# Routing steps of the attention stage at one per place instead of two, and the first expert's lower weight quarters all on GpSimd

## The chip, the cores and the metric

One Trainium2 chip, one of its cores. The metric is the device time of one execution in microseconds (us), lower is better. An execution's own time is a little longer than the span of its instructions, since something lies around them.

## What is computed

A linear attention with a per-channel decay (4 batches, 8 heads, 768 positions, 48 channels) whose result, read as 3072 rows of 384 values, goes through two layers of eight experts; each row takes the one expert with the largest logit.

```
for t in range(S):
    state = alpha[:, :, t, :, None] * state + np.einsum('bhd,bhe->bhde', k[:, :, t], v[:, :, t])
    y[:, :, t] = np.einsum('bhd,bhde->bhe', q[:, :, t], state)
...
h = np.maximum(xc[mask] @ w1[e], 0.0)
y[mask] = gate_w[mask, None] * (h @ w2[e])
```

The first layer skips rows whose score `x @ w_skip` is not positive and adds its result to the row; the second takes every row.

## The kernel before, in words

The attention is cut into NB = 24 chunks of 128 positions (6 per batch). The outer loop runs over g = 0 to 23, and an iteration g holds, in program order, work of several chunks:

- `emit_a(g + 1)`: 16 score matmuls of the next chunk into two PSUM banks (`ap`, L575), the causal mask for one bank by VectorE (L583) and for the other by ScalarE and GpSimd (L580, L581), then four transposes of the keys (`kp`, L590), which are left out where g + 1 is the last chunk of a batch.
- `prep(g + 3)`: two scans by VectorE over the decays with a reciprocal between them (L555, L557, L559), then two products by GpSimd (L563, L564).
- `emit_r(g - 1)`: eight matmuls (`rp`, L658) that give the rows and the logits of the chunk before; ScalarE copies the rows out and VectorE adds up the logits (`lg`, L661).
- `emit_y(g)`: the outputs (`yp`), from the masked scores (L612, L613) and from the carried state (L621, L622; left out where g is the first chunk of a batch), and the new state (`sp`, L617, L618, then `sa` by VectorE, L633, and four small copies by ScalarE, L636; left out where g is the last chunk of a batch).

The banks `ap` (two), `rp`, `sp` and `yp` come in turn out of one ring of four PSUM banks (tag "B"). An allocation takes the bank used four allocations earlier, so the second `ap` bank of an iteration is the `rp` bank of the iteration before, and is free once VectorE has made `lg`.

Engines take their instructions in program order. What TensorE runs is written out by hand in that order.

Rows are routed in groups of 6, 6, 6, 3 and 3 chunks (GROUPS). `route(i)` starts once the last chunk of its group has been through `emit_r`, that is in iterations 6, 12, 18, 21 and 23. It is a generator of small steps (softmax, choice of expert, rank within the expert, list of indices), nearly all VectorE instructions of 0.15 to 1 us, and it starts a second generator, `row_ends`, for counts, gates and a DMA of the row ends on SP's queue. `rt(n)` runs n steps, taken in turn from the active generators; `release()` lets a step go on that was left at a `yield 1` (the matmuls of rank, L322 to L325, and of the indices, L386). Calls of `rt` stand between the instructions of the attention: one in `emit_a` behind the mask, three in `prep`, three in `emit_r`, two in `emit_y`, and RT[g] at the end of the iteration (1 up to iteration 15). Two steps are heavy: `mv` (L374) and `hot` (L381), the latter followed by the index matmuls.

`finish` would run what is left of group i - 2 when group i starts.

From iteration 6, every second iteration ends with `background()`, one quarter of a split of the first expert's weights: ScalarE writes the f16 upper part (L205), then VectorE or GpSimd the bf16 lower part (`split_w`, L210). ON_POOL says which quarters GpSimd makes; for expert 0 these are quarters 0 and 2 of each of the two weights, so iterations 6, 10, 14 and 18 put one on GpSimd and 8, 12, 16 and 20 one on VectorE.

Behind the attention come the experts of the first layer and of the second, in which the weights of later experts are loaded into two raw buffers and split while TensorE works on the one before.

Of the kernel before, what the change touches and what calls it, by code (L numbers as in the profile page):

```python
# [47 lines left out]
SPLIT = 3  # L48
NWARM = 13

RT = [1, 1, 1, 1, 1, 1, 1, 1, 1, 1, 1, 1, 1, 1, 1, 1, 0, 2, 0, 2, 10, 10, 7, 14]

TURNS2 = ((0, 3), (1, 1), (1, 5), (2, 1))
REL3 = (2, 1, 3, 3, 3, 3, 3, 1, 1)
# [18 lines left out]
SPLITS2 = (((2, 0), (2, 2), (2, 4), (2, 6)), ((0, 3), (0, 6), (1, 3), (1, 6)))  # L73
TURNS = (((2, 1), (2, 3), (2, 5)), ((0, 1), (1, 1), (2, 1), (2, 4)))

ON_POOL = [(0, 2)] + [(1, 2, 3)] * 8 + [()] * 7

CST = {}
CW = 0
# [31 lines left out]
def body(tc, qka, vN, rw, wg2, wg17, w1a, w2a, w1b, w2b, cst, zr, out):  # L111
# [3 lines left out]
    with ctx:  # L115
# [21 lines left out]
        with ExitStack() as fctx, tc.manual_schedule():  # L137
# [8 lines left out]
            def bank(tag, name, *shape, parts=128):  # L146

                pool, bufs = phase.get(tag, (ps, 1))
                t = pool.tile([128, 512], F32, tag=tag, name=name, bufs=bufs)
                v = t[0:parts, 0:int(np.prod(shape))]  # L150
                if len(shape) == 2:
                    v = v.rearrange("p (a b) -> p a b", a=shape[0])
                elif len(shape) == 3:
                    v = v.rearrange("p (a b c) -> p a b c", a=shape[0], b=shape[1])
                return v
# [43 lines left out]
            def split_w(x, m, s):  # L199
# [5 lines left out]
                A.activation(out=hi[:, sl], in_=r[:, sl], func=AF.Copy)  # L205
                eng = P if s in ON_POOL[x] else V
                if x and s and eng is P and s - 1 not in ON_POOL[x]:

# [22 lines left out]
            def step(r):  # L231
                tok = next(r[0], None)
                if tok is None:
                    active.remove(r)
                else:
                    r[1] = turn[0] + (tok == 3) * LAG if tok in (1, 3) else None
                return tok != 2

            def rt(n=1):
                for _ in range(n):  # L240
                    for r in list(active):
                        if r[1] is None:
                            active.remove(r)
                            active.append(r)
                            if step(r):
                                break

            def release(w=1):
                turn[0] += 1
                for r in list(active):  # L250
                    if r[1] is not None and r[1] < turn[0] - w:
                        step(r)

            def start(gen):
                r = [gen, None]
                active.append(r)
                return r
# [292 lines left out]
            def prep(g, parts):  # L550

                a = at[g]
                pf = wk.tile([GP, AW], F32, tag="pp", name="pp", bufs=4)
                pp = pt[g] = pf.rearrange("p (a c) -> p a c", a=NP)
                V.tensor_tensor_scan(pf, a, bz, initial=0.0, op0=ALU.mult, op1=ALU.add)  # L555
                rt()
                V.reciprocal(bz.rearrange("p (a c) -> p a c", a=NP)[:, :, C + 1:], pp[:, :, C:C + 1])  # L557
                rt()
                V.tensor_tensor_scan(a[:, ::-1], a[:, ::-1], bz[:, ::-1], initial=0.0, op0=ALU.mult, op1=ALU.add)  # L559
                rt()  # L560
                iv = a.rearrange("p (a c) -> p a c", a=NP)[:, :, 2:]
                for c, ke, qe in parts:
                    ke.tensor_tensor(kt[g][:, c], kt[g][:, c], iv[:, c], op=ALU.mult)  # L563
                    qe.tensor_tensor(qt[g][:, c], qt[g][:, c], pp[:, c, 1:C + 1], op=ALU.mult)  # L564
# [30 lines left out]
            def emit_y(g):  # L595

                c = g % NC
                v, q = vt[g], qt[g]
                ta, tb = st.pop(("at", g, 0)), st.pop(("at", g, 1))
                y = st["ys", g] = wk.tile([YP, NP, C], F32, tag="y", name="y")  # L600

                n = 2 if g == NB - 1 else NP
                s = st.pop(("s", g)) if c else None
                step_s = c < NC - 1
                if step_s:
                    sp = bank("B", "sp", NP, D)
                for p0 in range(0, NP, n):
                    yp = bank("B", "yp", n, C, parts=YP)

                    for i in range(n):  # L610
                        p = p0 + i
                        T.matmul(yp[0:64, i, :], lhsT=v[:, p, 0:64], rhs=ta[:, p, :], start=(c == 0 or i == 0), stop=(c == 0))  # L612
                        T.matmul(yp[64:112, i, :], lhsT=v[:, p, 48:96], rhs=tb[:, p, :], start=(c == 0 or i == 0), stop=(c == 0))  # L613
                    if step_s:
                        ks = st.pop(("ks", g))
                        for p in range(NP):
                            T.matmul(sp[0:64, p, :], lhsT=ks[:, p, 0:64], rhs=v[:, p, 0:48], start=True, stop=True)  # L617
                            T.matmul(sp[64:128, p, :], lhsT=ks[:, p, 64:128], rhs=v[:, p, 48:96], start=True, stop=True)  # L618
                    for i in range(n if c else 0):
                        p = p0 + i  # L620
                        T.matmul(yp[0:48, i, :], lhsT=s[0:64, p, :], rhs=q[0:64, p], start=False, stop=(i == n - 1))  # L621
                        T.matmul(yp[64:112, i, :], lhsT=s[64:128, p, :], rhs=q[64:128, p], start=False, stop=(i == n - 1))  # L622
                    if n == NP:
                        free[0] = True
                        release()
                        free[0] = g >= NB - 2
                    A.activation(out=y[:, p0:p0 + n], in_=yp, func=AF.Copy)
                if step_s:
                    sn = wk.tile([GP, NP, D], F32, tag="s", name="s")
                    pp = pt.pop(g)  # L630
                    if c:
                        sa = wk.tile([GP, NP, D], F32, tag="sa", name="sa")
                        V.tensor_tensor(sa, sp, s, op=ALU.add)  # L633
                        sp = sa
                    for p in range(NP):
                        A.activation(out=sn[:, p, :], in_=sp[:, p, :], func=AF.Copy, scale=pp[:, p, C:C + 1])  # L636
                    st["s", g + 1] = sn
                    rt(2)
                if n < NP:
                    release()  # L640

# [7 lines left out]
            def emit_r(g):  # L649

                i, k, n, _ = gof[g]
                if k == 0:
                    xr[i] = em.tile([128, n, ROW - DM], F32, tag="xr", name="xr", bufs=3)
                y = st.pop(("ys", g))
                xy = em.tile([128, DM], F32, tag="xy", name="xy", bufs=4)
                rp = bank("B", "rp", NP, 113)
                for p in range(NP):
                    T.matmul(rp[:, p, :], lhsT=y[:, p, :], rhs=rws[:, p, :], start=True, stop=True)  # L658
                A.activation(out=xy.rearrange("p (a b) -> p a b", a=NP), in_=rp[:, :, 0:96], func=AF.Copy)
                A.dma_start(xrows[1 + g * 128:1 + (g + 1) * 128, 0:DM], xy)  # L660
                V.tensor_reduce(lg[:, g, :], rp[:, :, 96:113].rearrange("p a b -> p b a"), axis=AX.X, op=ALU.add)  # L661
                release()
                rt(3)

            def route(i):
                n = GROUPS[i]
# [84 lines left out]
            for i in range(NWARM):  # L751
                T.matmul(wm, lhsT=warm[:, 0:128], rhs=warm[:, 128:640], start=True, stop=True)
            prep(0, halves)
            prep(1, halves)
            emit_a(0)
            free[0] = False
            prep(2, halves)
            queue_split(0, 0)
            queue_split(0, 1)
            routes, orders = [], []  # L760
            for g in range(NB):
# [4 lines left out]
                if g > 0:  # L766
                    emit_r(g - 1)
                    i, k, n, _ = gof[g - 1]
                    if k == n - 1:
                        finish(*routes[max(i - 2, 0):max(i - 1, 0)])  # L770
                        routes.append(start(route(i)))
                emit_y(g)
                if g == 0:
                    A.activation(out=upper, in_=cc("upper"), func=AF.Copy)
# [20 lines left out]
                if g == NB - 1:  # L795
                    emit_r(g)
                    finish(*routes[:-1])
                    routes.append(start(route(len(GROUPS) - 1)))
                rt(RT[g])
                if g in (3, 6):  # L800
# [445 lines left out]
```

## Time and profile before

| | us |
|---|---|
| median of 3 runs | 523.43 |
| lowest, highest | 520.6, 524.15 |
| the profiled execution | 522.38 |
| its span | 520.7 |
| attention in it, up to the last `rp` matmuls | about 147 |

The profile is of one execution. PE is TensorE's matmuls, DVE VectorE, ACT ScalarE, POOL GpSimd, SP the engine whose queue issues loads. Times in the views count from the span's start. Matmuls are pipelined, so a matmul's own duration (about 0.27 us) is longer than the distance from one to the next.

### The profile page before, as it was taken

What the parts mean: (1) busy time and instruction counts of PE and PEld (TensorE: products, weight loads), DVE (VectorE), ACT (ScalarE), POOL (GpSimd) and SP (SyncE); (2) the same over time, 40 slices, a digit from 0 to 9 for tenths busy, and PEclk for the clock granted to TensorE, in tenths of its full rate; (3) what the DMA queues carried; (4) which work ended last, traced back from release to release, by engine and by line L of the source; (5) the groups of instructions that cost most, each with busy time, mean ns of one, the idle gap of its engine ahead of it and who ended that gap; (6) DMA issues with size and microseconds to landing.
All of it is one profiled execution on the core that took longest, in us unless ns stands there. A gap on an engine that the chain in (4) does not pass through costs nothing.

```text
span 520.7 us, 12000 instructions
## 1 busy us (share of the span) xinstructions
PE 488.2 (94%) x4669; PEld 377.1 (72%) x4669; DVE 347.0 (67%) x945; ACT 270.1 (52%) x546; POOL 246.3 (47%) x223
## 2 busy tenths in 40 slices
PE   5899998898989899999989989999999999999995
PEld 2788887787878899999988657565555566666663
DVE  7978888889577767877688745844636363636430
ACT  2465464564535666656566334744546364646430
POOL 2375655666526867797765253226115151402022
PEclk9899999999899999999999999999999999999998
DMA  8879786682345858677774167583544536271001
GB/s 295 293 263 334 260 260 205 189 272 52 77 155 169 284 181 276 222 261 263 248 253 139 35 237 255 172 273 88 162 147 155 172 108 230 67 258 40 7 34 43
DMA packets 44868, 96.74 MB, mean 186 GB/s; under 512 B 7049, under 2 KB 31879, under 8 KB 44806
## 3 DMA queue, kind: packets, MB, share of 16 engines
q1 hardware_dynamic: 36614, 77.68, 45.7%
q0 software_dynamic: 4736, 13.51, 7.7%
q10 hardware_dynamic: 3456, 4.72, 2.5%
q8 instruction: 39, 0.64, 0.5%
q14 instruction: 23, 0.19, 0.1%
HBM read 83.41 MB, written 12.99 MB: 185 GB/s over the span
## 4 chain that ended last, share of the span: by engine, by line
PE 52%; DVE 13%; DMA 6%; issue 5%; POOL 4%; ACT 3%; POOLq 0%; SPq 0%; DVEq 0%; ACTq 0%
PE hp L472 7%; PE hp L473 7%; PE hp L474 7%; DMA raw<-in_w1a 4%; PE ypc L496 4%; PE ypc L498 4%; PE ypc L497 4%; POOL w0l L210 3%; PE tp L459 2%; PE yp L497 2%; PE yp L498 2%; PE yp L496 2%; DMA raw<-in_w1b 1%; DVE qka L559 1%; DVE pp L555 1%
## 5 line engine op out<-in xcount | busy, mean ns | idle before, releaser
L996 POOL DMA_INDIRECT out<-o,ixo x31 | 32.4, 1046 | 140.0 <-ACT o L1071 117.7
L478 DVE SCALAR_TENSOR_TENSOR h2l<-hp,h2h 128x352 f16<-128x352 f32 (+8 forms) x66 | 38.7, 586 | 63.8 <-ACT h2h L477 63.1
L474 PE MATMUL hp<-x2h,w0l 128*128 128x352 f16 (+8 forms) x216 | 68.7, 323 | 0.0
L473 PE MATMUL hp<-x2l,w0h 128*128 128x352 f16 (+8 forms) x216 | 68.7, 323 | 0.0
L472 PE MATMUL hp<-x2h,w0h 128*128 128x352 f16 (+8 forms) x216 | 68.7, 323 | 0.0
L477 ACT ACTIVATE h2h<-hp 128x352 f16<-128x352 f32 (+8 forms) x66 | 33.8, 514 | 46.5 <-PE hp L474 46.4
L205 ACT ACTIVATE w0h<-raw 128x768 f16<-128x768 f32 x64 | 53.4, 836 | 7.2 <-DMA raw<-in_w1a 4.5
L472 PE MATMUL hp<-xh,w0h 128*128 128x200 f16 (+7 forms) x216 | 52.4, 252 | 2.4 <-DVE hl L478 1.5
L450 POOL DMA_INDIRECT xg<-xrows,ix x41 | 49.1, 1198 | 11.6 <-issue 9.5
L497 PE MATMUL yp<-hl,w1h 128*128 128x200 f16 (+7 forms) x216 | 52.6, 252 | 1.8 <-DVE hl L478 1.7
L473 PEld LDWEIGHTS <-w0h 128*128 128x128 f16 x432 | 42.3, 98 | 16.1 <-issue 2.8
L474 PEld LDWEIGHTS <-w0l 128*128 128x128 bf16 x432 | 42.3, 98 | 15.3 <-issue 0.4
L205 ACT ACTIVATE w1h<-raw 128x768 f16<-128x768 f32 x64 | 51.4, 836 | 3.6 <-DMA raw<-in_w2a 3.3
L496 PE MATMUL yp<-hh,w1h 128*128 128x200 f16 (+7 forms) x216 | 52.7, 252 | 0.4 <-ACT hh L477 0.4
L210 POOL TENSOR_TENSOR w1l<-raw,w1h 128x768 bf16<-128x768 f32 (+1 forms) x26 | 42.1, 1645 | 22.7 <-ACT w1h L205 12.3
L498 PE MATMUL yp<-hh,w1l 128*128 128x200 f16 (+7 forms) x216 | 52.6, 252 | 0.0
L473 PE MATMUL hp<-xl,w0h 128*128 128x200 f16 (+7 forms) x216 | 52.4, 252 | 0.1
L474 PE MATMUL hp<-xh,w0l 128*128 128x200 f16 (+7 forms) x216 | 52.4, 252 | 0.0
L472 PEld LDWEIGHTS <-w0h 128*128 128x128 f16 x432 | 42.3, 98 | 13.1
L563 POOL TENSOR_TENSOR qka<-qka 128x512 f32<-128x512 f32 (+1 forms) x24 | 27.5, 1147 | 49.3 <-DVE qka L559 44.1
L210 DVE TENSOR_TENSOR w0l<-raw,w0h 128x768 bf16<-128x768 f32 x38 | 37.8, 995 | 18.5 <-ACT w0h L205 16.4
L210 POOL TENSOR_TENSOR w0l<-raw,w0h 128x768 bf16<-128x768 f32 (+1 forms) x26 | 42.3, 1651 | 6.1 <-ACT w0h L205 4.8
(183 smaller groups left out, 1305.6 us busy)
## 6 DMA issues: line engine op xcount, KB each, us to landing
qka<-in_qka SPq DMA_DIRECT2D x21, 772.0 KB, 6.4
raw<-in_w1a SPq DMA_DIRECT2D x8, 1536.0 KB, 7.1
raw<-in_w2a SPq DMA_DIRECT2D x8, 1536.0 KB, 8.8
raw<-in_w1b SPq DMA_DIRECT2D x8, 1536.0 KB, 6.8
raw<-in_w2b SPq DMA_DIRECT2D x8, 1536.0 KB, 6.8
v<-in_vN SPq DMA_DIRECT2D x24, 192.0 KB, 5.0
xrows<-xy ACTq DMA_DIRECT2D x24, 192.0 KB, 4.0
xrows<-x SPq DMA_DIRECT2D x9, 197.0 KB, 6.1
```

What stands on the lines that cost most here:

```text
L205: A.activation(out=hi[:, sl], in_=r[:, sl], func=AF.Copy)
L210: eng.tensor_tensor(lo[:, sl], r[:, sl], hi[:, sl], op=ALU.subtract)
L450: P.indirect_dma_start(out=dst, out_offset=None, in_=xrows[0:rows], in_offset=bass.IndirectOffsetOnAxis(ap=ix, axis=0), bounds_check=rows ...
L472: T.matmul(hp[:, i], lhsT=wh[:, k, f], rhs=xh[:, k, 0:n], start=(k == 0), stop=False)
L473: T.matmul(hp[:, i], lhsT=wh[:, k, f], rhs=xl[:, k, 0:n], start=False, stop=False)
L474: T.matmul(hp[:, i], lhsT=wl[:, k, f], rhs=xh[:, k, 0:n], start=False, stop=(k == 2))
L477: A.activation(out=hh[:, f0:f0 + nf, 0:n], in_=hp, func=AF.Relu)
L478: V.scalar_tensor_tensor(out=hl[:, f0:f0 + nf, 0:n], in0=hp, scalar=0.0, in1=hh[:, f0:f0 + nf, 0:n], op0=ALU.max, op1=ALU.subtract)
L496: T.matmul(yp, lhsT=wh[:, f, ds], rhs=hs[0][:, f, c0:c1], start=(f == 0), stop=False)
L497: T.matmul(yp, lhsT=wh[:, f, ds], rhs=hs[1][:, f, c0:c1], start=False, stop=False)
L498: T.matmul(yp, lhsT=wl[:, f, ds], rhs=hs[0][:, f, c0:c1], start=False, stop=(f == 7))
L996: ins = P.indirect_dma_start(out=out, out_offset=bass.IndirectOffsetOnAxis(ap=ix, axis=0), in_=src, in_offset=None, bounds_check=N - 1, oo ...
```

## The change

`rt` is called less often in the first 17 iterations: RT[g] is 0 there, `emit_r` and `emit_y` run one step each instead of three and two, and `prep` two instead of three. From iteration 17 on all is as before. GpSimd makes all four lower quarters of both weights of expert 0.

```
-RT = [1, 1, 1, 1, 1, 1, 1, 1, 1, 1, 1, 1, 1, 1, 1, 1, 0, 2, 0, 2, 10, 10, 7, 14]
+RT = [0] * 17 + [2, 0, 2, 10, 10, 7, 14]
+
+EVEN = 17
...
-ON_POOL = [(0, 2)] + [(1, 2, 3)] * 8 + [()] * 7
+ON_POOL = [(0, 1, 2, 3)] + [(1, 2, 3)] * 8 + [()] * 7
...
                 V.tensor_tensor_scan(a[:, ::-1], a[:, ::-1], bz[:, ::-1], initial=0.0, op0=ALU.mult, op1=ALU.add)
-                rt()
+                if g >= EVEN + 3:
+                    rt()
...
                     st["s", g + 1] = sn
-                    rt(2)
+                    rt(1 if g < EVEN else 2)
...
                 release()
-                rt(3)
+                rt(1 if g + 1 < EVEN else 3)
```

## Rows read from the trace of the kernel before

**Rows 1.** Busy times of the engines, whole span

```profile
PE 488.2 (94%) x4669; PEld 377.1 (72%) x4669; DVE 347.0 (67%) x945; ACT 270.1 (52%) x546; POOL 246.3 (47%) x223
```

**Rows 2.** `rp` to `rp`: length; PE, PEld, DVE, ACT, POOL busy; clock, DMA share, GB/s

```profile
48.01:52.16 4.15, 3.97 (x58) 3.49 (x57) 3.91 (x10) 2.72 (x9) 2.28 (x4) 1.00 0.98 346
...
57.94:64.84 6.90, 5.81 (x85) 5.09 (x83) 6.21 (x18) 3.06 (x10) 3.22 (x4) 1.00 0.61 165
...
70.51:75.70 5.19, 5.19 (x76) 4.72 (x77) 4.21 (x8) 3.39 (x12) 4.48 (x5) 1.00 0.88 235
75.70:80.29 4.59, 4.59 (x63) 4.00 (x61) 3.33 (x6) 2.94 (x6) 4.48 (x5) 1.00 0.71 242
...
99.37:103.91 4.54, 4.54 (x74) 4.07 (x73) 3.06 (x6) 3.58 (x11) 3.20 (x3) 1.00 0.83 287
...
113.68:119.14 5.46, 4.57 (x62) 4.03 (x61) 5.21 (x12) 3.25 (x10) 4.58 (x5) 1.00 0.64 232
48.01:80.29 32.28, 30.44 (x431) 26.79 (x429) 27.33 (x62) 18.04 (x47) 20.37 (x21) 1.00 0.81 267
80.29:113.68 33.39, 30.13 (x436) 26.74 (x435) 28.05 (x62) 18.66 (x48) 18.27 (x18) 1.00 0.71 215
```

**Rows 3.** Waits of TensorE, 50 to 118 us: total, times, longest

```profile
PE ap L575 <- DVE lg L661: 1.9, 5, 0.6
PE idx_ps L386 <- DVE hot L381: 1.3, 2, 0.6
PE kp L590 <- DVE ad L327: 1.1, 1, 1.1
```

**Rows 4.** Waits of VectorE, 48 to 114 us

```profile
DVE w0l L210 <- ACT w0h L205: 2.6, 2, 1.8
DVE w1l L210 <- ACT w1h L205: 2.1, 1, 2.1
```

**Rows 5.** Timeline of iteration 16, no step in it: start, length, engine

```profile
102.82 1.16 PE L575 MATMUL ap<-qka 64*128 64x128 f32 x16
...
104.01 0.69 DVE L583 TENSOR_TENSOR at<-ap,cs 128x512 f32<-128x512 f32 x1 [1.51 <-PE ap L575]
104.62 1.23 DVE L555 TENSOR_TENSOR_SCAN pp<-qka,own 128x520 f32<-128x520 f32 x1
...
106.10 1.24 DVE L559 TENSOR_TENSOR_SCAN qka<-qka,own 128x520 f32<-128x520 f32 x1
107.26 0.20 DVE L661 TENSOR_REDUCE lg<-rp 128x17 f32<-128x68 f32 x1
```

**Rows 6.** Timeline of VectorE, steps of the first group

```profile
51.26 0.25 DVE L273 TENSOR_TENSOR sh<-lg,own 128x96 f32<-128x96 f32 x1
...
62.38 0.82 DVE L374 TENSOR_TENSOR mv<-on,own 128x192 f16<-128x192 f16 x2
63.11 0.95 DVE L381 TENSOR_TENSOR hot<-cs,own 128x768 f16<-128x768 f32 x1
63.98 0.35 DVE L633 TENSOR_TENSOR sa<-sp,s 128x192 f32<-128x192 f32 x1
```

**Rows 7.** Groups by line: the index matmuls, whole span

```profile
L386 PE MATMUL idx_ps<-mv,hot 128*128 128x96 f16 (+1 forms) x41 | 3.8, 202 | 3.5 <-DVE hot L381 3.5
```

**Rows 8.** Lower weight quarters, line L210: ns minimum/median/maximum, first and last start

```profile
L210 DVE TENSOR_TENSOR w0l<-raw,w0h x38: 951/958/2039, 66.1 to 478.6; 128x768 bf16<-128x768 f32 x38
...
L210 POOL TENSOR_TENSOR w0l<-raw,w0h x26: 1631/1648/1669, 52.8 to 279.7; 128x768 bf16<-128x768 f32 x18, 128x769 bf16<-128x769 f32 x8
```

**Rows 9.** Stretches in iterations 20 and 21, columns as in rows 2

```profile
130.00:132.00 2.00, 1.35 (x22) 1.16 (x21) 1.79 (x4) 0.17 (x1) 2.00 (x2) 0.99 0.51 92
132.00:133.00 1.00, 1.00 (x7) 1.00 (x6) 0.00 (x0) 1.00 (x5) 0.01 (x1) 0.50 0.00 0
...
135.00:136.00 1.00, 1.00 (x22) 1.00 (x20) 0.54 (x3) 0.40 (x2) 0.64 (x2) 0.82 0.00 0
```

**Rows 10.** The chain that ended last, 200 to 260 us

```profile
233.88 7.05 DMA raw<-in_w1a
```

## The prediction

> **What bounds the kernel now.** I read the page first: TensorE is busy for 94% of the span, VectorE for 67%, GpSimd for 47% [rows 1]. That is a mean over unlike stages, so I went to the stretches of the attention, cut where the `rp` matmuls of an iteration begin [rows 2]. Four of them show TensorE with no gap: 5.19 us with all its matmuls, 4.54 without the key transposes, 4.59 without a new state; the first iteration behind a batch (no carried state) takes 4.15. Six iterations of a batch are one of each of the last three and three full ones: 4.15 + 3 x 5.19 + 4.54 + 4.59 = 28.85. A group's rank and index matmuls come on top. The 41 index matmuls are busy for 3.8 us [rows 7], so six of them 0.56; with about 0.25 for the rank (an estimate from its seven like matmuls, mostly overlapped) the floor is 29.65 us. The two batches that carry the steps of groups 0 and 1 took 32.28 and 33.39 [rows 2], 2.6 and 3.7 above it. The first iteration of the next batch took 5.46, again 1.3 above the 4.15. So TensorE loses some 7.7 us here that the change can reach.
>
> The waits say to whom [rows 3]: to VectorE each time, for `lg` (it frees the bank of the next `ap`), for `hot`, for `ad`. And VectorE itself idles for ScalarE's upper halves, 2.6 and 2.1 us in the three quarters it makes up to 114 us [rows 4]: it stands in order behind a copy that ScalarE makes late. While this goes on GpSimd has work for 20.4 of 32.3 us and 18.3 of 33.4 [rows 2].
>
> The timeline of a quiet iteration gives the loop that matters [rows 5]. Scores begin at 102.82, the mask at 104.01, the scans follow, `lg` is done at 107.46, and only then the next scores can take their second bank: 4.6 us. A step between mask and `lg` lengthens the loop by its own duration. A step behind `lg` (the places in `emit_r` and `emit_y`) lies beside the 1.2 us that the next scores need until the mask can start, and costs nothing up to there, the 0.3 us of `sa` included. Against 5.19 the loop has 0.6 us to spare, against 4.54 none.
>
> **Part by part.** *The steps.* A group has 12 steps of `route` and 7 of `row_ends` by VectorE, plus two that `release` lets go. Calls per full iteration fall from 10 (one, three, three, two, one) to 5 (one, two, one, one, none), so a group that took iterations 6, 7 and 8, its indices at the start of 9, now takes 6 to 10, its indices at the start of 11. None is left for `finish` in iteration 18. Nothing is removed. A light step takes 0.15 to 0.3 us [rows 6]; `mv` takes from 62.38 to 63.11, 0.73, and with the small step before it 0.93; `hot` up to 63.98, 0.87. By the order of the calls:
>
> - Iteration 7: three light softmax steps between mask and `lg`, 3 x 0.29 = 0.87. Against 0.6 to spare TensorE loses 0.3. Before, it was four steps, and behind `lg` over 2 us.
> - Iteration 8: counts and gates, 0.28 + 0.48 + 0.2 = 0.96 in the same places, a loss of 0.35. Before, this iteration also ran `mv` and `hot` at one place, and its stretch took 6.90 [rows 2].
> - Iteration 9: the row ends, 0.25, and the rank; the loop is 4.85 against 4.54 plus the rank; nothing. `ad` now waits in VectorE's queue for the rank matmuls, with `sa` and two steps behind it; their followers are a mask that waits for the scores anyway and state copies due an iteration later. I take 0; the wait of 1.1 us that `ad` once caused [rows 3] bounds it, for `kp`, which is absent in this place.
> - Iteration 10: three light steps, 0.5, where there are no key transposes: 5.1 against 4.54, a loss of 0.55. Behind `lg` now stand `mv`, `sa` and `hot`, 0.93 + 0.28 + 0.87 = 2.1 us, while the scores take 1.1: the index matmuls wait 1.0 more. That wait does not go, it only moves (`hot` for 0.6 is in [rows 3]).
>
> A group then costs 0.3 + 0.35 + 1.55 = 2.2 us, two of them 4.4, and the first iterations of the two following batches, with the loop of 4.6 against 4.15, about 0.3 each: 5.0 to 5.1 in place of 7.7. The row ends' DMA waits on SP one iteration later than before, ahead of loads used two iterations on; I take 0.
>
> *The lower quarters.* Four leave VectorE, 0.96 us each, and with them the waits for ScalarE [rows 4, 8]. Their profit is inside the sum above, whose loops hold no quarter. The fourth, in iteration 20, is worth nothing: VectorE sits idle there for scores and rows that run at half clock [rows 9]. On GpSimd four come, 1.65 each [rows 8], 6.6 in all, in iterations 8, 12, 16 and 20; its busy time in a batch becomes some 22 of 32. A quarter there waits for ScalarE too, and behind it stand GpSimd's mask of the next chunk and its products for the chunk after; both are used one to two iterations later. I take 0 because iterations with a quarter on GpSimd ran without a gap (70.51 to 75.70 and 75.70 to 80.29, with 4.48 busy [rows 2]); if that cover is gone the price is up to 1.65 each. In iteration 20 the first gathers stand behind it too; their rows are wanted some microseconds later.
>
> The Trainium skill has a rule against the move ("SBUF — State Buffer", Who interferes with whom): a VectorE instruction with two SBUF inputs and a GpSimd instruction that reads SBUF shut each other out for a whole instruction. By it each new quarter could hold up VectorE by up to its own length, and the sum would turn to a loss. The rows have one such case: a VectorE quarter of 2.04 us instead of 0.96 [rows 8]. But the scans and nearly all steps read one operand from PSUM, so by the same rule they are exempt.
>
> *Sum.* 522.4 - (7.7 - 5.1) = 519.8 us by the profiled execution. That one lies 1.05 below the median of the runs shown, so 520.8 by the median; I give 520.3. What follows the attention depends on it by order and data, so all of it should come earlier by the same amount.
>
> **Rivals.**
>
> 1. *The steps cost nearly nothing when spread.* If VectorE's slack adds up over iterations rather than being lost in each, most of the 7.7 goes. For it: VectorE works 27.3 of 32.3 us [rows 2], and would have 2 us less to do. Against: each loop closes over `lg`, and a bank cannot be saved up. With 1.7 left, 522.4 - 6 = 516.4.
> 2. *The gain is lost behind the attention.* The chain passes through a weight load of 7.05 us [rows 10], the last of several. If loads, not TensorE, set that stage, an earlier start waits there: 522.4. Against: the loads are issued as buffers come free, so they move along.
> 3. *Slower: the clock falls in two more places.* In iterations 20 and 21 the granted clock is 0.50, the 1.2 GHz level, from 132.0 to about 135.4, after a stretch in which TensorE was busy for 1.35 of 2 us [rows 9]; 3.4 us at half speed lose 1.7. The new stall before the index matmuls in iterations 11 and 17 (0.55 and 1.0 within 2 us) looks much like that stretch. If the clock falls at both, 522.4 - 2.6 + 3.4 = 523.2; it decides from the point where these stalls are as long as in group 2. Against: stalls nearly as long in iterations 8 and 14 left the clock at 1.00 (57.94 to 64.84 [rows 2]). The Trainium skill ("TensorE: Matmul & The Clock Gate", HAM oscillation — how this bites in real kernels) says that waits between bursts of matmuls bring the clock down again and again; by it this rival, or its reverse, a fall in group 2 that no longer comes, is open here.
> 4. *GpSimd's quarters stretch VectorE or its own queue.* Four times 1.08 us, the excess of the 2.04 us case [rows 8]: 522.4 - 2.6 + 4.3 = 524.1. Against: GpSimd's busy iterations above.
>
> **How the numbers follow.** Forecast 0.50, with 517.5 to 522 as its own range; rival 1 0.20, rival 2 0.12, rival 3 0.10, rival 4 0.08. The range is 514.5 to 525: below, all 7.7 us gone, 514.7; above, rival 4 with the 1 us between the profiled run and the median. About 1% (5.2 us) is what a measurement tells from no change. Faster by more: most of rival 1 and a tenth of the forecast, 0.23. Slower by more: the tails of rivals 3 and 4 and what I have not seen, 0.07. Within: 0.70.
>
> **What would show it.** The timeline after should have groups 0 and 1 end in iterations 10 and 16, the two batches near 31.7 to 32 us each, TensorE's waits for `lg` smaller but the one for `hot` longer, no L210 on VectorE before the first expert, and `rp` of iteration 18 about 1.7 us and of 19 about 2.6 us earlier. The experts' stretches should keep their lengths. I am wrong if the batches come down to 30 (rival 1), if they do as forecast and the end does not move (2), if the clock shows 0.50 near iterations 11 or 17 (3), or if GpSimd is the releaser of TensorE or VectorE's instructions beside a quarter are longer (4).

## The result and the profile after

The changed kernel takes 516.46 us (median of 5 runs, 515.3 to 516.71) where the kernel before takes 520.69 (5 runs beside it): a ratio of 0.989, with a 95% interval of 0.9855 to 0.9926. By the two medians it is faster by 4.2 us, by the ratio 5.7, with the interval from 3.9 to 7.5. The prediction had 2.6 by the profiled execution, and 3.1 from the median that it knew (523.43; two runs more brought it to 520.69). The sign and the place were right, and 516.46 lies in the stated range, though below the forecast's own 517.5 to 522. The size was about half: the attention gained 5.03 where 2.6 was forecast.

First the busy times of the kernel after; VectorE has 3.7 us less than in [rows 1], GpSimd 6.2 more, TensorE 1.2 less:

```profile
PE 487.0 (95%) x4669; PEld 375.9 (73%) x4669; DVE 343.3 (67%) x941; ACT 270.8 (53%) x546; POOL 252.5 (49%) x227
```

Then the stretches from one iteration's first `rp` matmul to the next one's, of the kernel after, with the columns of [rows 2]: iterations 6, 7, 8, 10, 11 and 18, then 7 to 18 together, then 20 and 21.

```profile
47.25:51.94 4.69, 4.51 (x63) 4.04 (x61) 4.18 (x9) 3.39 (x9) 2.83 (x4) 1.00 0.96 346
51.94:57.03 5.09, 5.09 (x78) 4.62 (x77) 4.40 (x12) 3.16 (x10) 4.53 (x5) 1.00 1.05 405
57.03:62.77 5.74, 5.51 (x78) 4.86 (x77) 4.78 (x13) 3.27 (x9) 2.91 (x4) 1.00 0.61 208
...
67.65:73.38 5.73, 5.61 (x78) 4.95 (x77) 5.46 (x13) 2.54 (x8) 3.27 (x4) 1.00 1.00 386
73.38:78.22 4.84, 4.84 (x68) 4.29 (x67) 4.12 (x7) 3.58 (x9) 3.98 (x4) 1.00 0.81 254
...
109.20:113.89 4.69, 4.51 (x62) 4.03 (x61) 4.44 (x10) 3.26 (x10) 3.50 (x5) 1.00 0.69 248
51.94:113.89 61.95, 60.89 (x868) 54.20 (x867) 54.31 (x124) 37.50 (x95) 44.84 (x43) 1.00 0.75 250
119.76:127.05 7.29, 5.81 (x84) 5.08 (x83) 6.44 (x19) 3.18 (x11) 2.96 (x3) 1.00 0.26 58
127.05:131.60 4.55, 4.55 (x75) 4.08 (x73) 1.32 (x6) 3.76 (x10) 2.88 (x4) 1.00 0.13 45
```

The same cuts of the kernel before: iteration 6, 7 to 18 together, 20 and 21.

```profile
47.47:52.16 4.69, 4.51 (x63) 4.03 (x62) 4.45 (x11) 3.26 (x10) 2.82 (x4) 1.00 0.94 328
52.16:119.14 66.98, 61.17 (x868) 54.07 (x867) 56.68 (x125) 37.24 (x95) 40.95 (x40) 1.00 0.73 233
125.01:132.63 7.62, 6.14 (x85) 5.42 (x83) 6.44 (x19) 3.51 (x12) 2.96 (x3) 0.96 0.29 56
132.63:138.45 5.82, 5.82 (x74) 5.26 (x73) 3.41 (x14) 3.75 (x10) 3.14 (x4) 0.76 0.11 36
```

Iterations 7 to 18 took 66.98 us and take 61.95, 5.03 us less. Of these 4.75 were idle time of TensorE; its busy time changed by 0.28. All twelve, read from the same kind of rows (us):

| iteration | 7 | 8 | 9 | 10 | 11 | 12 | 13 | 14 | 15 | 16 | 17 | 18 |
|---|---|---|---|---|---|---|---|---|---|---|---|---|
| before | 5.78 | 6.90 | 5.67 | 5.20 | 4.58 | 4.69 | 7.37 | 7.02 | 4.54 | 5.18 | 4.58 | 5.47 |
| after | 5.09 | 5.74 | 4.87 | 5.74 | 4.84 | 4.69 | 5.10 | 5.74 | 4.87 | 5.74 | 4.84 | 4.69 |

Profile to profile the span falls by 5.9 us, from 520.7 to 514.8. Of this 0.22 is there before iteration 7, 5.03 comes in the table, and 1.6 between iteration 19 and the first expert. That last part is the clock: the stretches 125.01:132.63 and 132.63:138.45 of before ran at 0.96 and 0.76, those of after at 1.00. From the first expert's matmul on, after takes 0.95 longer (373.20 against 372.25). Neither of the two last terms can be put down to the change, as the second run of each kernel shows below.

TensorE's wait for `lg` in after, from 50 to 112 us, against [rows 3]; the index matmuls no longer stand in that view at all:

```profile
PE ap L578 <- DVE lg L664: 0.8, 4, 0.2
```

### The profile page after: what moved, and what is told of

It reads as the page before. It is cut to its first block, busy times and chain, and to the rows that moved or that the text cites. A ratio compares the mean times of both kernels' runs of the same rounds, so it can differ in the third digit from the quotient of the medians.

```text
span 514.8 us, 12005 instructions
## 1 busy us (share of the span) xinstructions
PE 487.0 (95%) x4669; PEld 375.9 (73%) x4669; DVE 343.3 (67%) x941; ACT 270.8 (53%) x546; POOL 252.5 (49%) x227
## 4 chain that ended last, share of the span: by engine, by line
PE 55%; DVE 21%; issue 7%; DMA 7%; POOL 5%; ACT 3%; POOLq 0%; DVEq 0%; ACTq 0%
PE hp L475 7%; PE hp L474 7%; PE hp L476 7%; DMA raw<-in_w1a 4%; DVE qka L561 4%; PE ypc L498 4%; DVE pp L557 4%; PE ypc L499 4%; PE ypc L500 4%; PE ap L578 3%; POOL w0l L212 3%; PE tp L461 2%; PE rp L661 2%; PE yp L624 2%; DMA raw<-in_w1b 1%
## 5 line engine op out<-in xcount | busy, mean ns | idle before, releaser
L480 DVE SCALAR_TENSOR_TENSOR h2l<-hp,h2h 128x352 f16<-128x352 f32 (+8 forms) x66 | 38.7, 586 | 63.8 <-ACT h2h L479 63.2
L212 POOL TENSOR_TENSOR w1l<-raw,w1h 128x768 bf16<-128x768 f32 (+1 forms) x28 | 45.4, 1648 | 24.6 <-ACT w1h L207 14.3
L499 PE MATMUL yp<-hl,w1h 128*128 128x200 f16 (+7 forms) x216 | 52.6, 252 | 1.8 <-DVE hl L480 1.7
L500 PE MATMUL yp<-hh,w1l 128*128 128x200 f16 (+7 forms) x216 | 52.6, 252 | 0.0
L212 POOL TENSOR_TENSOR w0l<-raw,w0h 128x768 bf16<-128x768 f32 (+1 forms) x28 | 45.7, 1654 | 5.5 <-ACT w0h L207 4.3
L212 DVE TENSOR_TENSOR w0l<-raw,w0h 128x768 bf16<-128x768 f32 x36 | 35.5, 986 | 15.9 <-issue 6.9
```

The source lines that it names most:

```text
L212: eng.tensor_tensor(lo[:, sl], r[:, sl], hi[:, sl], op=ALU.subtract)
L480: V.scalar_tensor_tensor(out=hl[:, f0:f0 + nf, 0:n], in0=hp, scalar=0.0, in1=hh[:, f0:f0 + nf, 0:n], op0=ALU.max, op1=ALU.subtract)
L499: T.matmul(yp, lhsT=wh[:, f, ds], rhs=hs[1][:, f, c0:c1], start=False, stop=False)
L500: T.matmul(yp, lhsT=wl[:, f, ds], rhs=hs[0][:, f, c0:c1], start=False, stop=(f == 7))
```

## The experiments

I had two theories of the 5.0 us. A: the main thing is the lower quarters, which stood in VectorE's order behind a late copy of ScalarE's. B: the heavy iterations were the loss, that is, the steps between mask and `lg` lengthen the loop of [rows 5], and spreading them shortens it, as forecast, with sizes off. The first two runs do one half of the change each. "7 to 18" below is always the stretch from iteration 7's first `rp` to iteration 19's.

**The spread alone** (the kernel after, with the quarters as before):

```diff
-ON_POOL = [(0, 1, 2, 3)] + [(1, 2, 3)] * 8 + [()] * 7
+ON_POOL = [(0, 2)] + [(1, 2, 3)] * 8 + [()] * 7
```

> Only the spreading of the steps; the quarters alternate as before. From the rp matmuls of iteration 7 to those of iteration 19 it takes 66.98 us before and 61.95 after. Theory A (the quarters hold VectorE up on their own, behind ScalarE's late copy): 64 to 65.5 here, so about 2 us of the 5.0 gained, the whole some 2 us faster than before plus or minus one fall of the clock (1.3 to 1.7 us). Rival B (the heavy iterations were the whole loss, and VectorE takes the quarters in its stride once the steps are spread): within 0.7 of 61.95.

Measured: 521.74 us, ratio 0.9981 [0.9953, 1.0008], which can't be told from the kernel before. Its stretches of iterations 9, 13 and 18, and 7 to 18:

```profile
62.74:68.98 6.24, 5.34 (x81) 4.63 (x79) 5.45 (x14) 3.11 (x8) 2.76 (x4) 1.00 0.41 72
...
84.05:91.12 7.07, 5.74 (x78) 4.84 (x77) 6.51 (x13) 3.41 (x10) 2.97 (x4) 1.00 0.65 214
...
112.17:118.02 5.85, 4.58 (x63) 4.04 (x61) 5.60 (x12) 3.26 (x10) 4.58 (x5) 1.00 0.52 191
51.91:118.02 66.11, 62.00 (x869) 54.69 (x867) 57.66 (x127) 37.59 (x95) 40.63 (x40) 1.00 0.68 235
```

And what VectorE's quarters wait for in it:

```profile
DVE w0l L212 <- ACT w0h L207: 2.2, 2, 1.7
DVE w1l L212 <- ACT w1h L207: 1.0, 1, 1.0
```

The spread alone saves 0.87 us of 66.98, less than the 2 that I expected by theory A. Where VectorE makes a quarter, an iteration takes 1.4, 2.0 and 1.2 us more than the same one of after (6.24 against 4.87, 7.07 against 5.10, 5.85 against 4.69): more than the 0.96 that the quarter lasts, since the wait of up to 1.7 comes on top.

**The quarters alone** (the same edit, made in the kernel before):

```diff
-ON_POOL = [(0, 2)] + [(1, 2, 3)] * 8 + [()] * 7
+ON_POOL = [(0, 1, 2, 3)] + [(1, 2, 3)] * 8 + [()] * 7
```

> Only the quarters on GpSimd; the steps as before. Iteration 7 to 19: 66.98 before, 61.95 after. Theory A: 63.5 to 64.5, about 3 us gained (0.8, 1.6 and 0.8 in the three stretches that follow a quarter on VectorE), and about 3 us in the whole. Rival B: 66 or more. If each part alone gives over 3.5, they overlap rather than add.

Measured: 519.05 us, ratio 0.9925 [0.9894, 0.9955]. Iterations 8 and 9, and 7 to 18:

```profile
57.66:64.56 6.90, 5.82 (x85) 5.09 (x84) 6.73 (x20) 3.06 (x10) 3.23 (x4) 1.00 0.63 173
64.56:69.10 4.54, 4.54 (x75) 4.07 (x73) 3.06 (x6) 3.58 (x11) 3.20 (x3) 1.00 0.75 263
...
51.88:115.22 63.34, 60.82 (x868) 54.05 (x867) 54.02 (x122) 37.21 (x95) 44.71 (x43) 1.00 0.75 245
```

The quarters alone save 3.64 us: iteration 9 falls from 5.67 to 4.54, TensorE without a gap, while iteration 8, with `mv` and `hot` in one place, keeps its 6.90 and TensorE its wait for `hot` (1.3 us as in [rows 3]). Theory A holds for most of the gain, which is a little more than I expected for it (63.34 against 63.5 to 64.5). The parts add up to 4.5, together they give 5.03.

**The index matmuls at the place where the prediction had them** (the kernel after; GpSimd, quarters and steps unchanged):

```diff
-                release()
+                release(0 if g in (12, 18) else 1)
```

> The changed kernel with the index matmuls of groups 0 and 1 let go one release earlier, behind the scores of iterations 11 and 17 instead of behind their rp. Theory (the predicted wait of 1.0 us for hot did not come because the matmuls stand 1.5 us further back): TensorE idles for hot by 0.6 to 0.9 us at each of the two places, iteration 7 to 19 takes 63.0 to 63.8 against 61.95. Rival (VectorE has hot done in time wherever they stand): no wait, 61.95.

Measured: 7 to 18 in 63.86 us, 1.91 more; time 521.39, a single run. Its iteration 10, and 7 to 18:

```profile
67.68:74.63 6.95, 5.91 (x85) 5.19 (x84) 6.68 (x15) 3.76 (x11) 3.91 (x4) 1.00 0.99 375
...
51.97:115.83 63.86, 60.97 (x869) 54.08 (x867) 54.29 (x124) 37.69 (x95) 44.92 (x43) 1.00 0.74 242
```

Its longest wait of TensorE:

```profile
PE idx_ps L388 <- DVE hot L383: 1.8, 2, 0.9
```

So 0.95 us a group, against the prediction's 1.0: the price was right, but the changed kernel doesn't pay it. (I had expected 63.0 to 63.8.)

**The kernel before once more, with its instructions' lines shifted** (three empty lines; nothing else):

> The kernel before, its lines shifted by three, once more with a profile. Theory (the fall of the clock in iterations 20 and 21 comes and goes between executions of the same kernel): the attention stretches repeat to 0.1 us up to iteration 20, and the clock may stay at 1.00 at 132 us; without a fall the execution takes about 520.6, with one 522.4 to 524. Rival (the fall belongs to the stall pattern of the kernel before): 0.50 from about 132 to 135.4 us again.

Measured: 523.82 us, a single run. Its 7 to 18, iterations 20 and 21:

```profile
53.35:120.33 66.98, 61.16 (x868) 54.06 (x867) 56.67 (x125) 37.25 (x95) 41.01 (x40) 1.00 0.74 239
126.20:133.49 7.29, 5.81 (x84) 5.08 (x83) 6.44 (x19) 3.18 (x11) 2.96 (x3) 1.00 0.26 58
133.49:138.03 4.54, 4.54 (x74) 4.07 (x72) 2.24 (x9) 4.03 (x11) 1.85 (x3) 1.00 0.13 45
```

Iterations 7 to 18 repeat to a hundredth. The clock's fall in iterations 20 and 21 is not there. The 520.6 us that I expected without it were missed all the same: iteration 7 begins 1.19 us later (53.35 against 52.16), and the part from the first expert on takes 374.11 against 372.25.

**The changed kernel once more**, unchanged:

> The changed kernel once more. The attention stretches should repeat to 0.1 us, 61.95 from iteration 7 to 19. Theory (the rest of the kernel varies by 1 to 2 us and with falls of the clock from one execution to the next, and the 0.95 us given back behind the attention belongs to that): the time from the first expert's first matmul to the end differs from the 373.2 us of the profile after, anywhere from 372 to 376. Rival (the change itself costs that stage 0.95 us): 373.2 again, to 0.2.

Measured: 517.22 us, ratio 0.9908 [0.9879, 0.9936]. Its 7 to 18, iterations 20 and 21, and two microseconds in them:

```profile
52.05:113.98 61.93, 60.88 (x868) 54.19 (x867) 54.26 (x124) 37.47 (x95) 44.77 (x43) 1.00 0.76 256
119.86:127.76 7.90, 6.42 (x84) 5.70 (x83) 6.43 (x19) 3.79 (x13) 2.95 (x3) 0.91 0.24 54
127.76:133.18 5.42, 5.42 (x73) 4.86 (x72) 2.60 (x13) 3.45 (x9) 4.08 (x4) 0.82 0.11 37
...
127.00:129.00 2.00, 2.00 (x12) 2.00 (x11) 0.00 (x0) 2.00 (x7) 0.51 (x1) 0.50 0.00 0
```

Now the changed kernel has the fall: the granted clock is 0.50, the 1.2 GHz level, and the two iterations take 13.32 where the first profile has 11.84. So the fall comes and goes in either kernel, and a profile of one against a profile of the other may show it as 1.5 us of gain or loss that the change has no part in.

**GpSimd's cover** (the kernel after; each quarter that the change moved to GpSimd is done twice there, with the same result):

```diff
-                eng.tensor_tensor(lo[:, sl], r[:, sl], hi[:, sl], op=ALU.subtract)
+                for _ in range(2 if x == 0 and s % 2 else 1):
+                    eng.tensor_tensor(lo[:, sl], r[:, sl], hi[:, sl], op=ALU.subtract)
```

> The changed kernel with GpSimd making each of the four moved quarters twice, 1.65 us more in iterations 8, 12, 16 and 20. Theory (GpSimd has cover; what stands behind a quarter there is used an iteration later): 61.95 to 62.3 from iteration 7 to 19. Rival (GpSimd's queue is close to the bound, so that the four quarters already cost something): 1 us or more per doubled quarter, 64.5 to 66.9.

Measured: 516.31 us, a single run; 7 to 18 unchanged, though GpSimd is busy for 49.20 us in it and not 44.84:

```profile
51.83:113.77 61.94, 60.68 (x869) 54.11 (x867) 54.27 (x124) 37.51 (x95) 49.20 (x46) 1.00 0.75 250
```

**The steps behind `lg`** (the kernel after; for groups 0 and 1 no step stands between mask and `lg`; the same steps are let go behind it):

```diff
-RT = [0] * 17 + [2, 0, 2, 10, 10, 7, 14]
+RT = [3] * 17 + [2, 0, 2, 10, 10, 7, 14]
...
-                rt()
+                if g >= EVEN + 3:
+                    rt()
...
-                        rt()
+                        if g > EVEN:
+                            rt()
```

(The second hunk stands at both places between the scans, the third in `emit_a`.)

> The changed kernel with the same number of steps per iteration up to 16, but none between the mask and lg: the three calls in emit_a and prep are gone there and three stand at the end of the iteration. Theory (the loop from scores to lg: a step in it costs its length beyond the spare, a step behind lg lies beside the next scores): the stretches 8 to 9 and 10 to 11, and 14 to 15 and 16 to 17, fall from 5.74 us to 5.1 to 5.3, and iteration 7 to 19 takes 60.0 to 60.8 against 61.95 after the change. Rival (what counts is VectorE's whole work in an iteration, wherever it stands): 61.95, within 0.4.

Measured: 515.62 us, ratio 0.9893 [0.986, 0.9926]; iterations 8 and 10, and 7 to 18:

```profile
56.88:61.92 5.04, 5.04 (x79) 4.57 (x77) 4.37 (x12) 2.96 (x10) 2.98 (x4) 1.00 0.70 257
...
66.79:72.41 5.62, 5.61 (x78) 4.95 (x77) 5.45 (x13) 2.54 (x8) 3.14 (x4) 1.00 0.95 321
...
51.85:112.04 60.19, 59.82 (x869) 53.51 (x867) 54.43 (x121) 37.43 (x95) 45.02 (x43) 1.00 0.78 259
```

Iteration 8 falls from 5.74 to 5.04, with as many steps per iteration as before, and TensorE is now without a gap: the forecast's mechanism, that a step between mask and `lg` costs and the same step behind `lg` doesn't, is borne out there. Iteration 10 goes only to 5.62, where I expected 5.1 to 5.3. In the whole time the 1.8 us can't be told: the intervals of this run and of the changed kernel beside it (516.46, 517.22) overlap.

**The same for the third group** (the run above, with the steps of iterations 17 to 19 in `RT` changed too):

```diff
-RT = [3] * 17 + [2, 0, 2, 10, 10, 7, 14]
+RT = [3] * 17 + [2, 4, 4, 10, 10, 7, 14]
```

> As e5_steps_behind, and group 2 spread further: four steps instead of none at the end of iteration 18, four instead of two at the end of 19. Its hot then stands at the end of iteration 20 and its index matmuls behind the rp of 21. Theory: the stretch 20 to 21 falls from 7.30 to 5.3 to 6 us, since TensorE no longer waits for hot, and the first expert starts 1 to 2 us earlier than in e5_steps_behind. Rival (the indices of group 2 are read, and the first rows gathered, later, and the first expert waits for them): the stretch falls and the first expert's start does not move, or moves back.

Measured: 515.75 us, ratio 0.988 [0.9848, 0.9911]. Iterations 19, 20 and 21:

```profile
112.16:119.07 6.91, 5.51 (x78) 4.85 (x77) 6.19 (x20) 3.18 (x9) 4.61 (x5) 1.00 0.11 32
119.07:124.44 5.37, 5.37 (x86) 4.84 (x84) 4.25 (x12) 3.10 (x10) 3.50 (x4) 1.00 0.47 114
124.44:130.49 6.05, 4.96 (x80) 4.36 (x78) 4.72 (x18) 3.32 (x8) 4.56 (x6) 1.00 0.12 39
```

Iteration 20 gains 1.9 us, 19 loses 1.0 (6.91 against 5.87), 21 loses 1.5: the first expert's matmuls start at 140.47, in the run above at 139.72. The wait moved, and nothing was gained.

**What holds iteration 10.** Two runs more, both from the run with the steps behind `lg`: `hot` one iteration later than `mv` (in the first of them only behind `lg` for one group), and then behind `lg` for both:

```diff
-RT = [3] * 17 + [2, 0, 2, 10, 10, 7, 14]
+RT = [3] * 10 + [0] + [3] * 5 + [0] + [2, 0, 2, 10, 10, 7, 14]
...
-                    rt(1 if g < EVEN else 2)
+                    rt(0 if g in (10, 16) else 1 if g < EVEN else 2)
```

> As e5_steps_behind, with hot taken away from mv: it stands one iteration later. In group 0 it comes behind lg of iteration 11, in group 1, by the call that is left in emit_a(18), between mask and lg of iteration 17. The same step at two places. Theory (a step behind lg is free up to about 1.2 us with sa, a step before lg costs its length beyond the spare): 10 to 11 and 16 to 17 fall from 5.6 to 5.1; 11 to 12 is 4.6, and 17 to 18 is 5.2 to 5.5. Rival (hot costs the same in both): 11 to 12 and 17 to 18 alike.

Measured: iterations 10 and 16 at 5.62 as before it, a miss; 11 at 4.81 and 17 at 5.06, where I had 17 at 5.2 to 5.5, another; 518.51 us, a single run. The second run's further edit:

```diff
-                        if g > EVEN:
+                        if g > EVEN + 1:
```

> As e9_hot_apart, with hot of group 1 behind lg of iteration 17 too. Theory: no stretch of iterations 7 to 18 with over 0.3 us above TensorE's own work, iteration 7 to 19 takes 58.9 to 59.4 us against 60.19 in e5_steps_behind and 61.95 after the change, and the whole is 2 to 3 us faster than after the change: 513.5 to 515, plus 1.3 to 1.7 for each fall of the clock. Rival (the experts behind do not follow): the stretches fall and the whole stays at 515.6 to 516.5.

Measured: 516.42 us, ratio 0.9871 [0.9835, 0.9906]; 7 to 18 in 60.03 where I expected 58.9 to 59.4, iteration 10 again 5.62, and the time above the 513.5 to 515 that I expected: misses too. In iteration 10 of this run no step stands between mask and `lg`, and `hot` stands an iteration later, so neither makes its excess; `mv` comes only behind the `lg` that TensorE waits for. VectorE's timeline shows a late mask:

```profile
67.31 0.26 DVE L329 TENSOR_TENSOR ad<-rk,ohm 128x96 f32<-128x96 f32 x1 [0.47 <-PE rk L327]
67.49 0.35 DVE L639 TENSOR_TENSOR sa<-sp,s 128x192 f32<-128x192 f32 x1
67.75 0.34 DVE L350 TENSOR_TENSOR on<-ohm,own 128x192 f16<-128x192 f16 x1
...
68.73 0.21 DVE L367 TENSOR_TENSOR own<-cs,own 128x48 f32<-128x48 f32 x1
68.85 0.68 DVE L588 TENSOR_TENSOR at<-ap,cs 128x512 f32<-128x512 f32 x1
```

`ad` waits 0.47 us for the rank matmuls, six further instructions stand behind it in order, and the mask, whose scores ended at 68.37 (67.21 + 1.16), starts at 68.85: 0.48 late, and it carries no wait of its own. That accounts for 5.62 against the 5.20 and 5.18 that iterations 10 and 16 take in the kernel before, where they hold no step.

In the changed kernel this is not so. There the same iteration reads:

```profile
66.55 1.16 PE L578 MATMUL ap<-qka 64*128 64x128 f32 x16
66.66 0.26 DVE L329 TENSOR_TENSOR ad<-rk,ohm 128x96 f32<-128x96 f32 x1 [0.34 <-PE rk L327]
...
67.75 0.69 DVE L586 TENSOR_TENSOR at<-ap,cs 128x512 f32<-128x512 f32 x1
68.36 0.17 DVE L360 TENSOR_TENSOR ge<-r,own 128x24 f32<-128x24 f32 x1
...
69.71 0.19 DVE L364 TENSOR_REDUCE own<-ge 128x6 f32<-128x24 f32 x1
...
70.15 0.21 DVE L367 TENSOR_TENSOR own<-cs,own 128x48 f32<-128x48 f32 x1
...
71.55 0.20 DVE L664 TENSOR_REDUCE lg<-rp 128x17 f32<-128x68 f32 x1
```

`ad` waits there too, but three steps fewer stand between it and the mask, which starts at 67.75, 0.04 behind the end of its scores. The three stand between mask and `lg` instead, and the way from mask to `lg` is 3.80 against 3.25 in [rows 5]: 0.55 longer, about what the three take (0.57). So in either place they cost some half microsecond: between mask and `lg` by their length, and behind `lg` because the wait of `ad`, `sa` and the steps ahead of them leave no room before the next mask. Whether the wait alone or the number of steps behind it is to be changed there, no run tells apart; a version with the rank matmuls apart from `ad` wasn't tried.

## Why the prediction was right in its sign and half in its size

*What bounds it* was right: the 7.7 us that TensorE lost over the floor, to VectorE, are what the change reached. 66.98 less two floors of 29.65 is 7.68. After it, 61.95 - 59.3 = 2.65 is left, where 5.0 to 5.1 was forecast. One row was misread on the way: 48.01:52.16 [rows 2] begins behind the first `rp` matmul (47.47), and that iteration takes 4.69, not 4.15; a full one takes 5.04 (the run with the steps behind `lg`), not 5.19. The two errors nearly cancel, which is luck: 4.69 + 3 x 5.04 + 4.54 + 4.59 + 0.81 = 29.75.

*The step that failed* is "the index matmuls wait 1.0 more", in iteration 10. They are let go only by the second release behind `hot`'s own `yield`, and so stand in TensorE's queue behind the next `rp`, not behind the scores; iteration 11 holds them and takes 4.84 without a gap. The run that puts them where the prediction saw them pays 0.95 a group. The 0.3 for each of the first iterations of the following batches fell too, but by the misread row: both take 4.69, the length that iteration 6 has without a step, and the loop of 4.6 fits into it. Together 2 x 1.0 + 2 x 0.3 = 2.6; the forecast left 2.4 too much in the attention.

*The other terms of the steps* came out in sum (1.2 forecast, 1.3 measured), not singly. Iteration 7: 0.3 forecast, 0.05 measured (5.09 against 5.04); its three steps lengthen the way from mask to `lg` by 0.60 (51.35 to 55.20 in after, 3.85 against 3.25), not by 0.87. Iteration 8: 0.35 forecast, 0.7 measured. Its loop, from the scores at 55.39 to the end of `lg` at 61.14, is 5.75 and not 5.56, since a scan also waits 0.20 for a product of GpSimd's, and what it has to be held against is 5.04, not 5.19:

```profile
57.72 1.24 DVE L557 TENSOR_TENSOR_SCAN pp<-qka,own 128x520 f32<-128x520 f32 x1 [0.20 <-POOL qka L567]
```

Iteration 9: 4.85 forecast, 4.87 measured. Iteration 10: 0.55 forecast, 0.56 measured (5.74 against 5.18 without a step), and for the reason forecast: three light steps between mask and `lg`, 0.55 by the timeline above. The price of 0 for the wait of `ad` was right for the changed kernel as well; only the runs with the steps behind `lg` pay for it.

*The quarters* were inside the sum, as "their profit", and with no number. They are the larger part: 3.64 us alone, against 0.87 for the spread alone. An engine's instruction of 0.96 us cost 1.2 to 2.0 because it stood in order behind another engine's late output, with the scans and `lg` behind it. That GpSimd takes them for nothing was right: twice as many moved quarters cost nothing either. That the fourth is worth nothing, as forecast, the spread alone shows: there VectorE still makes it behind a wait, and from iteration 19 to the first expert's matmuls it takes 27.67 us (118.02 to 145.69), as after does (113.89 to 141.56):

```profile
132.47 0.96 DVE L212 TENSOR_TENSOR w1l<-raw,w1h 128x768 bf16<-128x768 f32 x1 [1.81 <-ACT w1h L207]
```

*The rivals.* 1, the spread nearly free: 2.65 us are left where it had 1.7 and the forecast 5.1, so it was nearer the truth in the sum, but for its reason (slack that adds up over iterations) there is no sign: iterations 8 and 10 still pay, and 8 stops paying when its steps go behind `lg`. The two batches take 31.0 us each, between the 31.7 to 32 of the forecast and this rival's 30. That its 516.4 us is just what was measured is chance: of the 5.92 between the two profiled executions 1.6 is the clock's, and 0.95 went back behind the attention. 2, the gain lost behind the attention: the part from the first expert on took 372.25 and 374.11 in two profiles of before, 373.20 and 372.55 in two of after, so nothing is lost there that the repeats of one kernel don't show as well; the medians keep 4.2 us of the gain. 3, the clock in two more places: iterations 10, 11, 16 and 17 of after ran at 1.00. Its reverse, a fall in group 2 that no longer comes, is in the first pair of profiles, but by the repeats it belongs to neither kernel. 4, GpSimd's quarters in the way: refuted by the run that doubles them; VectorE's longest quarter now lasts 1.76 us against 2.04 in [rows 8], as this row of the quarters in after shows (minimum, median, maximum in ns):

```profile
L212 DVE TENSOR_TENSOR w0l<-raw,w0h x36: 949/959/1755, 151.5 to 472.8; 128x768 bf16<-128x768 f32 x36
L212 POOL TENSOR_TENSOR w0l<-raw,w0h x28: 1638/1655/1671, 52.6 to 274.0; 128x768 bf16<-128x768 f32 x20, 128x769 bf16<-128x769 f32 x8
```

The rule of the Trainium skill that spoke against the move ("SBUF — State Buffer", Who interferes with whom) stays without effect on the attention: with 4.4 us more of GpSimd's quarters in iterations 7 to 18, VectorE's busy time there is 54.27 against 54.31.

*What stays open:* why the 1.8 us that the runs with the steps behind `lg` gain in the attention don't show in their medians. Their profiles show where such a gain can go. The run with the steps behind `lg` and the one for the third group have a fall of the granted clock to 0.50 within the experts (256.0 to 259.4 and 255.8 to 259.2) that neither profile of the changed kernel has, and take 374.30 and 374.51 from the first expert on, against 373.20 and 372.55. The last run has none there, but its clock is at 0.50 up to 24.5 us, in after up to 16.3, and its iteration 7 begins 1.42 later (53.36 against 51.94). Whether their other executions lose it at the same places is not known. The first of these falls, in a cut of the run with the steps behind `lg`, and below it the same cut of after:

```profile
255.00:260.00 5.00, 3.80 (x26) 3.31 (x25) 4.34 (x18) 1.61 (x4) 2.61 (x3) 0.66 0.52 164
...
255.00:260.00 5.00, 3.52 (x38) 3.25 (x38) 4.49 (x19) 2.35 (x6) 4.13 (x4) 1.00 0.83 298
```

## What to carry to other kernels

An instruction that waits for another engine costs its engine the wait and all that stands behind it in order; where that order holds a ring together (scores, mask, scans, `lg`, next scores), even a short one belongs on an idle engine, or behind the instruction that closes the ring, as far as there is room before the next round (here the 1.2 us that the scores take). Before a wait is priced, find in the code which release lets the waiting instruction go: here one release more put the index matmuls half an iteration behind where they seemed to stand, and the wait was gone. And compare two profiles by stretches between the same events, with the stretches at a lower granted clock set apart, before a difference is put down to a change.

## What the runs showed of the hardware

Near iterations 20 and 21 the granted clock falls to 0.50 in 4 of 12 profiles (the kernel before, the quarters alone, the changed kernel once more, `hot` apart) and stays at 1.00 in the other 8, with the kernel before and the changed one on both sides, and costs 1.5 to 1.6 us. TensorE's gaps in iteration 20 are there without a fall too (5.81 busy of 7.29, in one profile of each kernel). The Trainium skill ("TensorE: Matmul & The Clock Gate", HAM oscillation — how this bites in real kernels) ties the falls to waits between bursts, and these iterations have such waits, in the profile of before the longest 0.83 us; that the same waits bring the clock down only at times is what these runs add.

The same coming and going is seen at three other places. At the start the clock stays at 0.50 up to 22.8 to 24.5 us in 3 of the 12 (the kernel before once more, `hot` apart and the run behind it), and iteration 7 begins there at 52.6 to 53.4 and not, as in the other 9, at 51.8 to 52.2. Behind the attention there are falls between 255 and 266 us in 4 of the 12 (the quarters alone, the index matmuls early, the steps behind `lg`, the third group) and near 160 in 2 (the quarters alone, `hot` apart). From the first expert on the 7 profiles with neither take 372.1 to 374.1 us, the 5 others 374.3 to 376.6.

The part behind the attention also holds a delay I can't place: ScalarE's third copy of `yth` in after starts at 157.56, 1.5 us behind its matmuls, with an idle time of 2.43 us that the profile puts down to `tp`. It isn't the change's: the second profile of before has it too (2.50 us), the first has 0.99 there, and the second of after has it (2.44) in a part that takes less, 372.55. Its cause is open.
